# Seven block products in place of eight in part of MLP1's first GEMM

## The chip, the cores and the metric

The kernel runs on one core of one Trainium2 chip. The metric is the device time of one execution in microseconds (us). TensorE (PE) multiplies, VectorE (DVE), ScalarE (ACT) and GpSimd (POOL) work on elements, and SyncE (SP) issues most transfers. SBUF and PSUM are the memories on the core; the eight PSUM banks (512 f32 columns on 128 partitions each) receive the products.

## The reference

Retention over 768 steps in 16 heads (two batches of eight) feeds two MLPs on 1536 tokens of width 512, with a hidden width of 2048:

```
state = gamma * state + k_t v_t^T ;  y_t = scale * q_t @ state          # per head
h = x @ w1_in  ; sp = log1p(exp(min(h, 20))) (h where h > 20)
x2 = (h * tanh(sp)) @ w1_out                                            # MLP1
h = x2 @ w2_in ; out = (h * cos(h)) @ w2_out                            # MLP2
```

All tensors are f32.

## The kernel before

**Retention** runs in six chunks of 128 tokens for each of the two batches: scores (L331), their mask (L337, DVE), the update of the state (L347), the new state `st` (L356, DVE), and the outputs in PSUM (L372, L382). POOL makes the decayed values `vd` (L309) and queries `qd` (L318, L321). ACT writes the high part of the outputs as `x` (L392), DVE the low part (L395).

**The MLPs.** An f32 operand is split into a high and a low part of a type that TensorE multiplies at full rate, and each product is made of three terms (high·high, high·low, low·high). An MLP is worked in four groups of 512 hidden columns and three tiles `j` of 512 tokens. For a group and a tile, `gemm1` (L419) makes h in four column slices of 128 (48 matmuls), two slices together being a *pair* of two banks; Mish (L456, ACT), the high part (L486, ACT) and the low part (L490, DVE) make `g`; `gemm2` (L447) multiplies it by the group's second weight (48 matmuls), and the result is added to `acc` (L506, DVE).

**Weights** come as items: `w(i,G,u)` is half u of group G's part of the first weight, `w(o,G,u)` of the second. An item is loaded into `raw` (L210, SP) and split: absolute value (`mag`; L215 on ACT for the first item, else L222 on DVE), clamp (L228), exponent (L232), rounded high value with its sign (L238), copy of the high part (L250, ACT), the difference (L256, DVE) and the low part (L264, on DVE for the early items, later on POOL). The early items are split in two halves, n0 and n1, of 128x512 each; two `raw` buffers exist, so item k+2 is loaded once item k's low part is done.

**Order.** A class `Plan` list-schedules all operations by costs written beside them and issues each engine's instructions in that order. Engines work in order; on the chip an instruction waits only for semaphores of the data and buffers that it touches. `hold(a, b)` gives the planner a time before which `a` is not placed; it makes no semaphore. Names of buffers in the trace: `bank` is PSUM, `wi` and `wo` weights.

Of the kernel before, what the change touches and what calls it, by code (L numbers as in the profile page):

```python
# [34 lines left out]
    (("x", 2, 0), ("x", 2, 1)), (("wi", 1), ("wi", 2)), (("g", 0), ("g", 1)),  # L35
    (("wo", 0), ("wo", 1)), (("wo", 2), ("g", 2)), (("wi", 2), ("g", 0)),
# [10 lines left out]
TERMS = ((0, 0), (0, 1), (1, 0))  # L47

# [126 lines left out]
def retention_two_mlps(ctx: ExitStack, tc: tile.TileContext, qkv, w1i, w1o, w2i, w2o, consts, out):  # L175
# [9 lines left out]
    t_p = ctx.enter_context(tc.tile_pool(name="t", bufs=3))  # L185
# [207 lines left out]

    def att_x_low(c, b):
        nc.vector.tensor_sub(out=x_chunk(c, b, 1), in0=att_y(c, b), in1=x_chunk(c, b, 0).bitcast(F32))  # L395


# [5 lines left out]
    g_t = {}  # L403

# [48 lines left out]
    def mish(k, fs=slice(0, 2)):  # L453
        if fs.start == 0:
            t_t[k] = t_p.tile([128, 2, BLK], F32, tag="t", name="mish")
        nc.scalar.activation(out=t_t[k][:, fs], in_=h_of(k, fs), func=AF.Mish)  # L456


    def cos_turns(k):
        t_t[k] = t_p.tile([128, 2, BLK], F32, tag="t", name="turns")  # L460
        nc.scalar.activation(out=t_t[k], in_=h_of(k), func=AF.Identity, scale=INV_2PI, bias=quarter)  # L461

    def cos_whole(k):
        n_t[k] = k_p.tile([128, 2, BLK], F32, tag="k", name="whole")
        nc.scalar.activation(out=n_t[k], in_=t_t[k], func=AF.Identity, bias=magic)  # L465

    def cos_angle(k):
        t = t_t[k]
        nc.vector.scalar_tensor_tensor(  # L469
            out=t, in0=n_t[k], scalar=MAGIC, in1=t, op0=ALU.subtract, op1=ALU.subtract  # L470
        )

    def cos_clamp(k):
        t = t_t[k]
        nc.vector.tensor_scalar(out=t, in0=t, scalar1=-0.5, scalar2=0.5, op0=ALU.max, op1=ALU.min)  # L475

    def cos_sin(k):
        nc.scalar.activation(out=t_t[k], in_=t_t[k], func=AF.Sin, scale=-TWO_PI)  # L478

    def g_mul(k):  # L480
        nc.vector.tensor_mul(out=t_t[k], in0=t_t[k], in1=h_of(k))  # L481

    def g_high(k, late):
        n = len(g_t) % 5
        g_t[k] = (late_p if late else g_p).tile([128, 2, 2, BLK], F32R, tag="g%d" % n, name="g")
        nc.scalar.copy(out=g_t[k][:, :, 0, :], in_=t_t[k])  # L486

    def g_low(k):
        g = g_t[k]
        nc.vector.tensor_sub(out=g[:, :, 1, :], in0=t_t[k], in1=g[:, :, 0, :].bitcast(F32))  # L490
# [38 lines left out]
    at = {"gs": []}  # L529

    def weight(it, between=lambda: None):
        raw, mag, w = ("raw", it), ("mag", it), ("w", it)
        first, single = it == ("i", 0, 0), it[:2] in (("i", 0), ("o", 0), ("i", 1))
# [6 lines left out]
        for load, ns in zip(loads, [slice(0, 1), slice(1, 2)] if single else [slice(0, 2)]):  # L540
            c = 0.55 if single else 1.0
            new = None if ns.start else (mag, 2)
            if first:
# [30 lines left out]
            for n in range(ns.start, ns.stop):  # L574
                at["w", it, n] = last

# [26 lines left out]

    def chunk_pre(c):
        for b in range(B):
            if c + 1 < NCH:
                vd = ("vd", c, b)
                op(None, 0.0, att_vd_new, c, b, new=(vd, 2, "vd%d" % b))
# [46 lines left out]
    def chunk_inter(c):  # L655
# [6 lines left out]
        for b in range(B):  # L662
# [6 lines left out]
            at["xl", c, b] = low = op("DVE", 0.69, att_x_low, c, b, needs=[high], uses=[y, x])  # L669
            at.setdefault(x, []).append(low)  # L670
            at.setdefault(("high",) + x, []).append(high)

    def tile_in(m, G, j, f, parts=range(KD), only=None):
# [16 lines left out]
        t, g = ("t", k), ("g", k)  # L690
        if m == 0:
            last = op("ACT", 1.06, mish, k, needs=[last, table], new=(t, 3), uses=hs)
        else:
            kk = ("k", k)
            last = op("ACT", 1.12, cos_turns, k, needs=[last], new=(t, 3), uses=hs)
            last = op("ACT", 1.06, cos_whole, k, needs=[last, at["close"]], new=(kk, 2), uses=[t])
            last = op("DVE", 1.27, cos_angle, k, needs=[last], uses=[t, kk])
            last = op("DVE", 0.72, cos_clamp, k, needs=[last], uses=[t])
            last = op("ACT", 1.08, cos_sin, k, needs=[last], uses=[t])
            last = op("DVE", 1.25, g_mul, k, needs=[last], uses=[t] + hs)  # L700
        n = len(at["gs"]) % 5
        at["gs"].append(k)
        last = op(
            "ACT", 1.06, g_high, k, n > 2, needs=[last] + ([at["close"]] if n > 2 else []),
            new=(g, 1, "g%d" % n), uses=[t],
        )
        at["g", k] = op("DVE", 1.27, g_low, k, needs=[last], uses=[t, g])

    def tile_out(m, G, j, d, u, cols=slice(0, DM)):
# [6 lines left out]
            "PE", 0.72 if half else 1.36, gemm2, m, G, j, d, u, cols, needs=[at[w + (0,)], at[g], at["close"]],  # L716
# [10 lines left out]
        if G == 0:  # L727
            last = op("ACT", 1.05, out_first, m, G, j, p, needs=[last], uses=os + [acc], new=None if p else (acc, NJ))
# [12 lines left out]
    acc_p = k_p = late_p = None  # L741
# [6 lines left out]
    def close():  # L748
        nonlocal acc_p, k_p, late_p
        att_stack.close()  # L750
        acc_p = ctx.enter_context(tc.tile_pool(name="acc", bufs=NJ))
        k_p = ctx.enter_context(tc.tile_pool(name="k", bufs=2))
        late_p = ctx.enter_context(tc.tile_pool(name="late", bufs=1))
# [48 lines left out]
    at["close"] = op(None, 0.0, close)  # L802
    op("PE", 5.5, start_up)
# [21 lines left out]
    later = {1: [("o", 0, 0)], 2: [("o", 0, 1)], 3: [("i", 1, 0)], 4: [("i", 1, 1)]}  # L825
# [22 lines left out]
    for c in range(1, NCH):  # L848
        hold(at["xh", c, 1], at["xh", c, 0])
        if 1 < c < NCH - 1:  # L850
            hold(at["vd", c, 0][1], at["xh", c - 1, 1])
            hold(at["vd", c, 1][1], at["vd", c, 0][1])
    for f in range(2):
        for x in terms:
            tile_in(*steps[0], f, whole, x)
    for i, f in ((1, 0), (1, 1), (0, 2), (0, 3), (1, 2), (1, 3)):
        tile_in(*steps[i], f)
    plan.ops[at["close"]]["before"] |= {n for n, o in enumerate(plan.ops) if o["att"]}
    def weights_of(i):
# [78 lines left out]
```

## Time and profile before

| | us |
|---|---|
| median of 3 runs | 571.11 (570.95 to 571.59) |
| profiled execution | 571.46 |
| its span (first to last instruction) | 569.7 |
| TensorE busy | 564.1 (99% of the span) |
| DVE / ACT / POOL busy | 383.7 / 225.4 / 95.7 |

The profiled execution is 1.76 us longer than its span, and 0.35 us longer than the median. The MLPs begin at 44.01 us of the span.

### The profile page before, as it was taken

How to read it: one execution, taken by the hardware profiler on the slowest of the kernel's cores; microseconds unless marked ns; L12 is line 12 of the kernel's file. 1: busy time of each engine (PE TensorE's matmuls, PEld its weight loads, DVE VectorE, ACT ScalarE, POOL GpSimd, SP SyncE). 2: the span in 40 equal slices, each digit the busy share in tenths (PEclk: the TensorE clock that was granted, in tenths of full speed). 3: DMA queues.
4: the chain of work that ended last, by engine and by line, in shares of the span. 5: the costliest groups of instructions: out<-in, count | busy, mean ns of one | idle time of the engine just before them, and what ended most of it. 6: DMA issues, size and time to landing. Idle time of an engine off the chain costs nothing.

```text
span 569.7 us, 7217 instructions
## 1 busy us (share of the span) xinstructions
PE 564.1 (99%) x3052; PEld 469.1 (82%) x3052; DVE 383.7 (67%) x417; ACT 225.4 (40%) x259; POOL 95.7 (17%) x66
## 2 busy tenths in 40 slices
PE   8999999999999999999999999999999999999997
PEld 7888888888888888888888888888888888888886
DVE  6679899652465527563487976898498894765462
ACT  4264443331312302304326466366246354354240
POOL 6760001111110201111101111122010311010000
PEclk9999999999999999999999999999999999999999
DMA  8983054421042100312021120404003100000203
GB/s 291 396 320 147 3 198 171 148 102 47 1 147 75 74 1 4 144 74 75 0 75 74 49 100 1 147 0 148 0 1 147 41 34 2 0 1 0 75 37 112
DMA packets 16160, 49.32 MB, mean 87 GB/s; under 512 B 1792, under 2 KB 2176, under 8 KB 16128
## 3 DMA queue, kind: packets, MB, share of 16 engines
q1 hardware_dynamic: 16128, 48.86, 23.5%
q8 instruction: 24, 0.39, 0.3%
q14 instruction: 8, 0.07, 0.0%
HBM read 45.71 MB, written 3.15 MB: 86 GB/s over the span
## 4 chain that ended last, share of the span: by engine, by line
PE 96%; DMA 3%; SPq 0%; issue 0%; DVE 0%
PE bank L447 46%; PE bank L419 46%; DMA qkv<-qkv_dram 3%; PE bank L372 1%; PE bank L331 1%; PE bank L382 1%; PE bank L347 1%; SPq L296 0%; SPq L758 0%; DVE acc L513 0%
## 5 line engine op out<-in xcount | busy, mean ns | idle before, releaser
L419 PE MATMUL bank<-x,wi 128*128 128x512 f32 x1152 | 264.8, 389 | 0.0
L419 PEld LDWEIGHTS bank<-x,wi 128*128 128x128 f32 x1152 | 216.1, 188 | 45.0 <-issue 0.2
L447 PE MATMUL bank<-wo,g 128*128 128x512 f32 (+2 forms) x588 | 132.7, 385 | 0.0
L447 PE MATMUL bank<-g,wo 128*128 128x512 f32 x576 | 132.3, 389 | 0.0
L447 PEld LDWEIGHTS bank<-wo,g 128*128 128x128 f32 x588 | 109.1, 188 | 22.1
L447 PEld LDWEIGHTS bank<-g,wo 128*128 128x128 f32 x576 | 108.1, 188 | 22.5
L490 DVE TENSOR_TENSOR g<-mish,g 128x1024 fp32r<-128x1024 f32 x24 | 33.5, 1394 | 58.0 <-ACT g L486 57.9
L264 POOL TENSOR_TENSOR wo<-mag,wo 128x1024 fp32r<-128x1024 f32 x14 | 35.5, 2534 | 214.6 <-ACT wo L250 206.8
L506 DVE TENSOR_TENSOR acc<-bank,acc 128x1024 f32<-128x1024 f32 x35 | 42.8, 1222 | 34.6 <-PE bank L447 34.4
L456 ACT ACTIVATE mish<-bank 128x1024 f32<-128x1024 f32 x24 | 24.7, 1029 | 96.5 <-PE bank L419 96.5
L264 POOL TENSOR_TENSOR wi<-mag,wi 128x1024 fp32r<-128x1024 f32 x12 | 30.3, 2527 | 192.9 <-ACT wi L250 192.9
L469 DVE SCALAR_TENSOR_TENSOR turns<-whole,turns 128x1024 f32<-128x1024 f32 x24 | 29.4, 1223 | 44.7 <-ACT whole L465 44.7
L461 ACT ACTIVATE turns<-bank,quarter 128x1024 f32<-128x1024 f32 x24 | 26.7, 1114 | 65.4 <-PE bank L419 65.1
L238 DVE SCALAR_TENSOR_TENSOR mag<-raw,mag 128x1024 uint32<-128x1024 uint32 (+1 forms) x38 | 40.1, 1056 | 1.1
L478 ACT ACTIVATE turns<-turns 128x1024 f32<-128x1024 f32 x24 | 25.5, 1062 | 34.8 <-DVE turns L475 34.6
L490 DVE TENSOR_TENSOR g<-turns,g 128x1024 fp32r<-128x1024 f32 x24 | 33.2, 1383 | 8.0 <-ACT g L486 8.0
L481 DVE TENSOR_TENSOR turns<-turns,bank 128x1024 f32<-128x1024 f32 x24 | 29.2, 1216 | 10.1 <-ACT turns L478 6.8
L256 DVE SCALAR_TENSOR_TENSOR mag<-raw,mag 128x1024 uint32<-128x1024 uint32 x26 | 33.7, 1301 | 0.4
L486 ACT CAST g<-turns 128x1024 fp32r<-128x1024 f32 x24 | 25.1, 1045 | 17.0 <-DVE turns L481 16.9
L250 ACT CAST wi<-mag 128x1024 fp32r<-128x1024 f32 (+1 forms) x20 | 17.5, 874 | 27.5 <-DVE mag L256 22.4
L465 ACT ACTIVATE whole<-turns,magic 128x1024 f32<-128x1024 f32 x24 | 27.7, 1153 | 0.8
L232 DVE TENSOR_SCALAR mag<-mag 128x1024 uint32<-128x1024 uint32 (+1 forms) x38 | 27.0, 710 | 1.1
(51 smaller groups left out, 320.8 us busy)
## 6 DMA issues: line engine op xcount, KB each, us to landing
raw<-w1i_dram SPq DMA_DIRECT2D x16, 512.0 KB, 4.2
raw<-w1o_dram SPq DMA_DIRECT2D x16, 512.0 KB, 4.1
raw<-w2i_dram SPq DMA_DIRECT2D x16, 512.0 KB, 3.7
raw<-w2o_dram SPq DMA_DIRECT2D x16, 512.0 KB, 3.7
qkv<-qkv_dram SPq DMA_DIRECT2D x12, 512.0 KB, 7.7
qkv<-qkv_dram SPq DMA_DIRECT2D x22, 256.0 KB, 7.2
out_dram<-acc SPq DMA_DIRECT2D x11, 256.0 KB, 2.1
out_dram<-acc SPq DMA_DIRECT2D x1, 160.0 KB, 1.8
```

The source lines that it names most:

```text
L232: nc.vector.tensor_scalar(out=a, in0=a, scalar1=3, scalar2=0x3FFFFFF8, op0=ALU.logical_shift_left, op1=ALU.bitwise_and)
L238: nc.vector.scalar_tensor_tensor(out=a, in0=high, scalar=0xC0000000, in1=a, op0=ALU.bitwise_and, op1=ALU.bitwise_or)
L256: nc.vector.scalar_tensor_tensor(out=w_all_of(it, single)[:, ns], in0=raw_t[it][:, ns, :, 0], scalar=29, in1=mag_t[it][:, ns], op0=ALU.log ...
L264: eng.tensor_sub(out=w[:, :, 1], in0=w_all_of(it, single)[:, ns].bitcast(F32), in1=w[:, :, 0].bitcast(F32))
L419: nc.tensor.matmul(h, w[:, f % 2, a, kk * 128 : (kk + 1) * 128], x[:, b, kk, :], start=(a + b + kk == 0), stop=(a == 1 and kk == KD - 1),)
L447: nc.tensor.matmul(ps, lhs, rhs, start=(n == 0), stop=(n == 3 * GF - 1))
L461: nc.scalar.activation(out=t_t[k], in_=h_of(k), func=AF.Identity, scale=INV_2PI, bias=quarter)
L465: nc.scalar.activation(out=n_t[k], in_=t_t[k], func=AF.Identity, bias=magic)
L469: nc.vector.scalar_tensor_tensor(out=t, in0=n_t[k], scalar=MAGIC, in1=t, op0=ALU.subtract, op1=ALU.subtract)
L481: nc.vector.tensor_mul(out=t_t[k], in0=t_t[k], in1=h_of(k))
L490: nc.vector.tensor_sub(out=g[:, :, 1, :], in0=t_t[k], in1=g[:, :, 0, :].bitcast(F32))
L506: nc.vector.tensor_add(out=acc, in0=o_of((m * NG + G, j, p)), in1=acc)
```

## The change

In groups 1 to 3 of MLP1, token tiles 0 and 1 and one pair of column slices are taken as a 2 by 2 block problem with K halved (Winograd's form of Strassen's scheme): seven products of 6 matmuls (L495) take the place of eight (48 matmuls in all). There are six such blocks; tile 2 of these groups and all of group 0 stay as they were. The scheme needs four sums S1 to S4 of blocks of x and four sums T of blocks of each weight item, split in high and low parts like the operands, and additions of the products in PSUM. The core of the diff:

```diff
+WINOGRAD = (
+    ("c", ("x", 0, 0), ("w", 0, 0), False), ("d", ("S", 2), ("T", 2), False), ("a", ("S", 1), ("T", 0), False),
+    ("b", ("S", 3), ("T", 1), False), ("c", ("x", 0, 2), ("w", 0, 2), True), ("a", ("x", 1, 0), ("w", 1, 2), True),
+    ("b", ("x", 1, 2), ("T", 3), True),
+)
...
+    def w_first_differences(it):
+        w = mag_t[it].bitcast(F32)
+        nc.gpsimd.tensor_sub(
+            out=t_of(it)[:, 0:2], in0=w[:, 1].rearrange("p (k n) -> p k n", k=2), in1=w[:, :, 0 : DM // 2]
+        )
...
+    def att_y_copy(c, b):
+        for k in (0,):
+            y_whole(b, k)
+            nc.scalar.copy(out=att["y"][:, b, :, c * C : c * C + C], in_=att_y(c, b))
...
+    def s_op(to, a, b, plus):
+        to, a, b = (tmp[t] if isinstance(t, int) else y_whole(*t) for t in (to, a, b))
+        (nc.gpsimd.tensor_add if plus else nc.gpsimd.tensor_sub)(out=to, in0=a, in1=b)
...
+    def wino(gi, p, n):
+        to, x, w, more = WINOGRAD[n]
+        ps, last = bank[:, WINO_BANK[to], :], len(TERMS) - 1
+        for kk in range(2):
+            for i, (a, b) in enumerate(TERMS):
...
+                nc.tensor.matmul(
+                    ps, lhs, rhs, start=(not more and kk + i == 0), stop=(kk == 1 and i == last), skip_group_check=True
+                )
...
+    def wino_add(to, n, of):
+        to = tmp[3][:, to] if isinstance(to, int) else bank[:, WINO_BANK[to], :]
+        nc.vector.tensor_add(out=to, in0=bank[:, WINO_BANK[of], :], in1=tmp[3][:, n])
...
-    def mish(k, fs=slice(0, 2)):
-        if fs.start == 0:
-            t_t[k] = t_p.tile([128, 2, BLK], F32, tag="t", name="mish")
-        nc.scalar.activation(out=t_t[k][:, fs], in_=h_of(k, fs), func=AF.Mish)
-
+    def mish(k):
+        nc.scalar.activation(out=h_of(k), in_=h_of(k), func=AF.Mish)
...
-            if first:
+            if it[:2] == ("o", 0) or first:
                 at["act", it, ns.start] = last = op("ACT", 0.62, w_abs_act, it, ns.start, needs=[load], new=new, uses=[raw, mag])
...
-    later = {1: [("o", 0, 0)], 2: [("o", 0, 1)], 3: [("i", 1, 0)], 4: [("i", 1, 1)]}
+    later = {1: [("o", 0, 0)], 2: [("o", 0, 1)]}
...
+    s1 = sum_of(1, (1, 0), (1, 2), True)
+    s2 = sum_of(2, 1, (0, 0), False, s1)
+    s3 = sum_of(3, (0, 0), (1, 0), False)
+    s4 = sum_of((0, 2), (0, 2), 2, False, s2)
+    hold(s1, at["w", ("i", 0, 1), 1])
+    hold(s3, s2)
...
+    for G in range(1, NG):
+        mini(G, 0)
+        g_split()
+        tiles_out(0, G - 1, 2)
...
+        mini(G, 1)
+        g_split()
...
+        tiles_out(0, G, 0)
+        tiles_in(0, G, 2, range(GF))
+        tiles_out(0, G, 1)
```

Around it: ACT copies eight chunks of the retention's output as f32 (`y`, L450 of the changed kernel); Mish works in place in PSUM, so that a pair's banks come free after the low part of g instead of after Mish; the absolute values of `w(o,0,0)` and `w(o,0,1)` move from DVE to ACT; the weights of group 1 are loaded later; some SBUF buffers share slots.

**POOL at the end of the retention.** Before, behind the last `vd` and `qd` (`cst` holds the decays), POOL has nothing to do until the first low part of a weight of group 0's second half:

```order
L309 TENSOR_TENSOR vd<-qkv,cst 128x256 [waits DMAHW6_49,Activation_49]
L309 TENSOR_TENSOR vd<-qkv,cst 128x256 [waits DMAHW7_49,Activation_49]
L321 TENSOR_TENSOR qd<-qkv,cst 64x512 [waits DMAHW5_49,PE_49,Pool_49]
L321 TENSOR_TENSOR qd<-qkv,cst 64x512
L264 TENSOR_TENSOR wo<-mag,wo 128x2x512 [waits PE_49,DMAHW0_49,Activation_49,Pool_49]
```

In the changed kernel the four sums (L471; `tmp`, `y` and `uw` are f32 buffers) stand directly behind them:

```order
L360 TENSOR_TENSOR vd<-qkv,cst 128x256 [waits DMAHW7_49]
L368 TENSOR_TENSOR qd<-qkv,cst 128x512 [waits DMAHW3_49]
L471 TENSOR_TENSOR tmp<-y 128x1024 [waits PE_49,Activation_49,Pool_49]
L471 TENSOR_TENSOR tmp<-tmp,y 128x1024 [waits Pool_49]
L471 TENSOR_TENSOR y<-y,tmp 128x1024 [waits Pool_49]
L471 TENSOR_TENSOR uw<-y 128x1024
L484 TENSOR_TENSOR S<-tmp,S 128x1024 [waits DVE_49,PE_49,Activation_49] x2
```

None of the four waits for DVE: the first waits for PE (the last update of the state, whose `vd` had the slot), for ACT (the last `y` copy) and for POOL itself.

**ACT at the first pairs.** Before, behind the splits of the first item, Mish and the high part of g alternate with copies of weights:

```order
L250 CAST wi<-mag 128x512 x2
L456 ACTIVATE mish<-bank 128x1024
L486 CAST g<-mish 128x2x512
L250 CAST wi<-mag 128x512
L456 ACTIVATE mish<-bank 128x1024
L486 CAST g<-mish 128x2x512
L250 CAST wo<-mag 128x512
```

In the changed kernel an absolute value of `w(o,0,0)` stands ahead of the first Mish (L578) and another ahead of the second, each between two table loads:

```order
L267 CAST wi<-mag 128x512
L228 ACT_TABLE_LOAD
L228 ACTIVATE mag<-raw 128x512
L578 ACT_TABLE_LOAD
L578 ACTIVATE bank<-bank 128x1024
L628 CAST g<-bank 128x2x512
L267 CAST wi<-mag 128x512
L228 ACT_TABLE_LOAD
L228 ACTIVATE mag<-raw 128x512
L578 ACT_TABLE_LOAD
L578 ACTIVATE bank<-bank 128x1024
L628 CAST g<-bank 128x2x512
```

A third such stretch follows (load, absolute value, copy of S, absolute value, load, third Mish). The program has nine table loads; before it had three.

**PE in groups 0 and 1.** Before, 48 matmuls of each GEMM alternate from here on:

```order
L419 MATMUL bank<-x,wi 128x512 x48
L447 MATMUL bank<-g,wo 128x512 x48
L419 MATMUL bank<-x,wi 128x512 x48
L447 MATMUL bank<-g,wo 128x512 x48
L419 MATMUL bank<-x,wi 128x512 x48
```

In the changed kernel the first 144 matmuls of gemm1 (now L543) and 96 of gemm2 (now L571) are as they were, and then come the two blocks of group 1, each of seven products:

```order
L543 MATMUL bank<-x,wi 128x512 x144
L571 MATMUL bank<-g,wo 128x512 x96
L495 MATMUL bank<-x,wi 128x512 x6
L495 MATMUL bank<-S,T 128x512 x18
L495 MATMUL bank<-x,wi 128x512 x12
L495 MATMUL bank<-x,T 128x512 x6
L571 MATMUL bank<-g,wo 128x512 x48
L495 MATMUL bank<-x,wi 128x512 x6
L495 MATMUL bank<-S,T 128x512 x18
L495 MATMUL bank<-x,wi 128x512 x12
L495 MATMUL bank<-x,T 128x512 x6
```

A block of two tiles takes 42 matmuls, where two pairs took 48.

## Rows read from the trace of the kernel before

**Rows 1.** The page: busy time of each engine, share of the span, instructions.

```profile
PE 564.1 (99%) x3052; PEld 469.1 (82%) x3052; DVE 383.7 (67%) x417; ACT 225.4 (40%) x259; POOL 95.7 (17%) x66
```

**Rows 2.** Chain of waits: start us, length us, engine, buffer, line, instructions.

```profile
44.01 32.88 PE bank L419 x144
...
98.65 10.88 PE bank L419 x48
...
544.73 22.13 PE bank L447 x108
566.88 0.36 DVE acc L513
```

**Rows 3.** Timeline, 38 to 55 us: start, length, operation, [idle before, releaser].

```profile
38.94 1.10 PE L347 MATMUL bank<-vd,qkv 128*64 128x64 f32 x32
...
40.70 0.68 DVE L238 SCALAR_TENSOR_TENSOR mag<-raw,mag 128x512 uint32<-128x512 uint32 x1
...
45.67 0.69 DVE L264 TENSOR_TENSOR wi<-raw,wi 128x512 fp32r<-128x512 f32 x1 [0.50 <-ACT wi L250]
...
46.39 7.57 SPq L210 DMA_DIRECT2D raw<-w1o_dram  x4
...
49.73 1.03 ACT L456 ACTIVATE mish<-bank 128x1024 f32<-128x1024 f32 x1 [1.18 <-PE bank L419]
...
54.84 1.22 DVE L490 TENSOR_TENSOR g<-mish,g 128x1024 fp32r<-128x1024 f32 x1
```

**Rows 4.** Timeline where DVE and POOL work together: 380 us, 96 us.

```profile
379.94 1.22 DVE L238 SCALAR_TENSOR_TENSOR mag<-raw,mag 128x1024 uint32<-128x1024 uint32 x1
379.98 3.44 POOL L264 TENSOR_TENSOR wo<-mag,wo 128x1024 fp32r<-128x1024 f32 x1 [8.92 <-ACT wo L250]
...
381.19 3.30 DVE L256 SCALAR_TENSOR_TENSOR mag<-raw,mag 128x1024 uint32<-128x1024 uint32 x1
...
95.86 2.48 POOL L264 TENSOR_TENSOR wo<-mag,wo 128x1024 fp32r<-128x1024 f32 x1 [56.14 <-ACT wo L250]
96.13 2.77 DVE L232 TENSOR_SCALAR mag<-mag 128x1024 uint32<-128x1024 uint32 x1
```

**Rows 5.** Groups by line and shape, DVE: busy us, mean ns of one.

```profile
L256 DVE SCALAR_TENSOR_TENSOR mag<-raw,mag 128x1024 uint32<-128x1024 uint32 x26 | 33.7, 1301 | 0.4
L238 DVE SCALAR_TENSOR_TENSOR mag<-raw,mag 128x1024 uint32<-128x1024 uint32 x26 | 31.8, 1224 | 0.8
L232 DVE TENSOR_SCALAR mag<-mag 128x1024 uint32<-128x1024 uint32 x26 | 21.9, 841 | 0.7
L228 DVE TENSOR_SCALAR mag<-mag 128x1024 f32<-128x1024 f32 x26 | 18.0, 692 | 0.5
L222 DVE TENSOR_SCALAR mag<-raw 128x1024 uint32<-128x1024 uint32 x26 | 17.4, 687 | 3.9 <-POOL wo L264 3.8
L337 DVE TENSOR_TENSOR p<-bank,cst 128x512 f32<-128x512 f32 x24 | 15.0, 682 | 3.1 <-PE bank L331 3.1
```

**Rows 6.** The same view, POOL and ACT.

```profile
L264 POOL TENSOR_TENSOR wo<-mag,wo 128x1024 fp32r<-128x1024 f32 x14 | 35.5, 2534 | 214.6 <-ACT wo L250 206.8 <-DMA raw<-w1o_dram 7.8
L486 ACT CAST g<-mish 128x1024 fp32r<-128x1024 f32 x24 | 25.2, 1050 | 1.3 <-PE bank L447 0.6
L250 ACT CAST wi<-mag 128x512 fp32r<-128x512 f32 x8 | 5.0, 620 | 5.1 <-DVE mag L238 5.1
```

**Rows 7.** Timeline: ACT's first absolute value of n1 and a table load.

```profile
38.05 0.69 ACT L215 ACTIVATE mag<-raw 128x512 f32<-128x512 f32 x1 [0.78 <-DMA raw<-w1i_dram]
38.77 1.28 ACT L451 ACT_TABLE_LOAD   x1
```

**Rows 8.** Loads into `raw` issued from 40 to 62 us: issue to landing.

```profile
DMA to landing us min/median/max: 3.2/3.7/4.1
```

**Rows 9.** Timeline of PE at the program's start (matmuls of zeros).

```profile
1.06 5.30 PE L793 MATMUL bank<-zero 128*128 128x256 bf16 x24 [1.06 <-DVE magic L798]
...
8.52 1.06 PE L793 MATMUL bank<-zero 128*128 128x256 bf16 x8
```

More of the change, by code (lines that the diff above doesn't have):

```diff
@@ L669, in chunk_inter @@
             at["xl", c, b] = low = op("DVE", 0.69, att_x_low, c, b, needs=[high], uses=[y, x])
+            if c < 4:
+                at["yc", c, b] = op("ACT", 0.58, att_y_copy, c, b, needs=[high], uses=[y])
             at.setdefault(x, []).append(low)
@@ L689, in tile_in @@
             return
-        t, g = ("t", k), ("g", k)
+        g = ("g", k)
         if m == 0:
[L692 to L707, printed above, removed]
+            at["g"].append((k, [op("ACT", 1.06, mish, k, needs=[last, table], uses=hs)], hs))
+            return
+        n = len(at["cos"])
+        at["cos"].append(k)
+        t, kk = ("t", k), ("k", k)
@@ L859, in weights_of @@
[L859 to L881 removed]
+            tile_in(0, 0, 0, f, whole, x)
@@ new lines, in retention_two_mlps, with sum_of @@
+    g_split()
+    tiles_in(0, 0, 1, (0, 1))
+    tiles_in(0, 0, 0, (2, 3))
+    last_j1 = len(plan.ops)
+    tiles_in(0, 0, 1, (2, 3))
+    j1_done = [n for n in range(len(plan.ops)) if plan.ops[n]["fn"] is gemm1 and plan.ops[n]["args"][2] == 1]
+    new = op(None, 0.0, s_new, needs=[at["ret"]], new=[("S", 1, "S2"), ("tmp", 1, "T")])
+    plan.lines["UW"], plan.lines["S1"], plan.lines["S3"] = ["S"], ["S"], ["S"]
+    sums = ["S", "tmp"]
+    def sum_of(to, a, b, plus, *after):
+        return op("POOL", 2.0, s_op, to, a, b, plus, needs=[new, *after], uses=sums)
@@ new lines, in split_of @@
+    def split_of(n, last, *after):
+        uses = sums + ([("x", 0, 1)] if n == 4 else [])
+        high = op("ACT", 1.05, s_high, n, needs=[last, *after], uses=uses)
+        at["S", n] = [op("POOL", 2.4, s_low, n, needs=[high], uses=uses)]
+    s1 = sum_of(1, (1, 0), (1, 2), True)
[4 more added lines that the diff above has]
+    hold(s3, s2)
+    for n, last in ((2, s2), (1, s1), (3, s3)):
+        split_of(n, last)
@@ L883, in retention_two_mlps @@
+    at["t"] = op(None, 0.0, t_new, new=[("turns", 1, "S2"), ("turns2", 1, "UW"), ("whole", 1, "S3")])
+    plan.lines["S1"] = ["S"]
+    free_g.append(4)
+    last = (0, NG - 1, 2)
+    for i, step in enumerate(steps[NG * NJ :]):
+        m, G, j = step
+        if j < 2:
+            weights_of(m * NG + G, j)
+        tiles_in(*step, range(GF))
+        tiles_out(*last, by_pairs)
+        last = step
+    tiles_out(*last, in_the_end)
     with tc.manual_schedule():
```

301 lines of the change are left out of this document (229 added, 72 removed).

## The prediction

> **What bounds the kernel now.** I read the page's busy times first: TensorE works 564.1 of 569.7 us [rows 1]. The chain of waits says the same in order of time: from 44.01 us to 566.86 us it is PE alone, one GEMM phase of 48 matmuls after another at 10.88 us, so 226.7 ns per matmul, and 0.36 us of DVE end it [rows 2]. No other engine is near its limit on average. So a matmul less is 226.7 ns less, as long as what PE reads is ready and its banks are free. The place where this is tightest is found in the timeline behind 44 us: PE begins the MLPs while the first weight item is still being split on DVE (n0's and n1's operations run from 40.70 to 46.36 us), and the load of `w(o,0,0)` goes out at 46.39, when the first `raw` is free [rows 3].
>
> **What the change removes.** Six blocks of 48 matmuls become 42: 36 x 226.7 ns = **-8.16 us** on PE [rows 2].
>
> **The sums and DVE.** The four sums (128x1024 on POOL) stand directly behind the retention's last `qd`, and none waits for DVE. The planner's `hold` places them behind the split of `w(i,0,1)` in its plan only. Their last release is the end of PE's last update: 38.94 + 1.10 = 40.04 us [rows 3]. So they run from about 40.1 us, just when DVE has to make n0 and n1 of the first item. I price a sum by POOL's low part of the same size, 2534 ns, less some waiting in that mean: 2.4 to 2.5 us [rows 6].
>
> What does such an operation do to DVE? The rows at 380 us show both engines wanting their SBUF operands at once: L238 runs 1.22 us undisturbed, POOL's L264 is issued at 379.98 and shows 3.44 us, its own 2.4 plus a wait for L238's end; then L256, next on DVE, shows 3.30 us in place of some 1.2. At 96 us L232 shows 2.77 us where its mean is 0.84 [rows 4, 5]. So one operation waits for the whole of the other, and the one that asked first goes next: POOL got in between two neighbours on DVE. With four sums back to back each lets one DVE operation through: first sum 40.1 to 42.5, L256's part of n0 to 43.2; second to 45.6, clamp of n1 to 46.0; third to 48.4, exponent of n1 to 48.9; fourth to 51.3, rounding of n1 to 52.0 (DVE operations at 0.4 to 0.7, as at 128x512 in [rows 3]). Then low n0 ends at 52.7, difference and low n1 at 54.0. Without the sums, in this order, low n1 would end at 45.4: **8.6 us late**. PE's first pair needs low n0 in its third term, after 8 matmuls at 45.8 us, and low n1 two matmuls later; so PE stands still until 54.0 and is 7.7 us late (54.0 + 0.45 of the two matmuls against 46.72).
>
> The Trainium skill, SBUF — State Buffer, section "Who interferes with whom", calls the port pair that DVE and GpSimd share an exclusive lock, taken by DVE operations with two SBUF inputs or in a 2-port mode. The trace agrees in [rows 4]; the page doesn't say who gets it next.
>
> **The table loads on ACT.** The order shows six more ACT_TABLE_LOADs around the absolute values of `w(o,0,0)` and `w(o,0,1)`, now on ACT. One takes 1.28 us and starts at once behind the operation before it [rows 7]. ACT works in order, so the first Mish stands behind a transfer. The first `raw` comes free with low n1 (54.0), the load lands 3.2 us later at best [rows 8]: 57.3. Load of the table 58.6, absolute value (0.69) 59.3, table 60.5, Mish (1.03) 61.6, high part (1.05) 62.6, low part on DVE (1.22) 63.85 [rows 3, 6, 7]. Mish now works in the banks, so only then are the first pair's banks free for the third pair: PE starts it at 64.0, where it was 44.01 + 48 x 0.2267 = 54.9: 9.1 us late, already more than the 7.7 above. The fourth pair waits for copy 0.62, load 1.28, absolute value 0.69, load 1.28, Mish, high, low from 62.6 on: 70.0 (before 60.3). The fifth waits for two copies of S (1.05 each), two absolute values, two loads, Mish, high, low from 68.7 on: 78.2 (before 65.8). From there on ACT has no such stretch, and the pairs follow PE again: group 0's first GEMM ends at 89.3 in place of 76.89. In all PE loses **12.4 us**, some 8.6 by the sums and 3.8 by ACT. Two absolute values on ACT save DVE's L222 there, which is on nobody's path.
>
> The Trainium skill, ScalarE: Activation LUTs, section "Table sets: the hidden batching unit", says that cheap functions such as abs are in every set. By that no load would be needed between Abs and Mish, and the time would be that of the third rival below. The trace shows one behind an absolute value, ahead of Mish's first use [rows 7], and the order has them in the program; that each costs its 1.28 us there, no row shows.
>
> **PE's clock.** At the start 24 small matmuls took 5.30 us (221 ns each), and 8 later ones 1.06 us (133 ns) [rows 9]: the lower level (1.2 GHz) and most of the higher (2.4). A pause of 8 us may bring the lower one back. At worst the first 24 units of work afterwards cost 24 x 88 ns = 2.1 us more; the first two pairs would end at 64.7 in place of 62.6, where the third waits for ACT until 64.0 anyway. I take 0, bound 0.7.
>
> **What lies beside other work.** The eight `y` copies (as the 0.62 us copies, [rows 6]) stand on ACT in the retention, where PE waits for transfers: 0, at most 0.6 if the last of them delays the last chunk. In each block the seven products take 1.36 us each. The first add into a bank that PE returns to must be done in the two products between (2.72 us), and costs 0.68 as L337, which reads PSUM likewise [rows 5]: 2.0 us to spare; the next, 1.8. The T parts of an item (POOL 1.3, 0.6, 0.6, 2.5; ACT 1.05) come out about 3 us before their block in group 1 and 8 in the others. The four copies and low parts of S run until about 85 us, before their first use at about 111. MLP2 and the tail keep their order: 0.
>
> The narrowest place is the second half of `w(o,G,·)`: its `raw` is free only after the low part of T. From there, landing 3.7 (up to 4.1), DVE 0.69 + 0.69 + 0.84 + 1.22 + 1.30, copy 1.05, POOL 2.53 make 12.0 us [rows 5, 6, 8], where I count 14.4 until PE asks for it. I take 0; with two more waits like those of [rows 4] it is 2 to 3 us in each of three groups.
>
> **The sum.** 571.46 - 8.16 + 12.4 = 575.7 for an execution like the profiled one, which is 0.35 over the median of the runs: **575.3 us**. Its own range: the landings 3.2 to 4.1, each sum 2.3 to 2.5, the order in which the two engines get in (one operation of 0.7 more or less in two places) and the clock: 573.5 to 577.5.
>
> **The rivals.**
> - *DVE gets through* (faster, the other side). If DVE, whose operations follow each other within 0.1 us, keeps its operands until low n1 is done, POOL waits instead and nobody needs the sums before 62 us. Only ACT's 3.6 us stay (load out at 45.4, landing 48.6; third pair at 55.3, fifth at 69.4 against 65.8): 571.46 - 8.16 + 3.6 - 0.35 = 566.6. It speaks for it that the sums also wait for each other; against it, that L264 got in between L238 and L256 [rows 4]. It decides below 8.16 - 3.6 = 4.6 us of delay: when at most one sum of four gets in ahead.
> - *Half of it.* Two sums get in ahead: 3.6 + 4.3 = 7.9 us lost, 570.9 and so no change to speak of.
> - *The table loads cost nothing*, because none is needed between an absolute value and Mish, or because it is done during the wait for the transfer. With the sums in the way as above, PE is late by the 7.7 us of low n1: 571.46 - 8.16 + 7.7 - 0.35 = 570.7, the same. (The first of these reasons is the rule of the page ScalarE: Activation LUTs of the Trainium skill, cited above.)
> - *Neither costs:* 571.11 - 8.16 = 563.0.
> - *The second halves of w_out late as well:* 575.3 + 5 = 580, if the 2.4 us to spare go in two groups.
> - That fewer matmuls are not run is excluded by the order: 42 stand where 48 were.
>
> **How the numbers follow.** The forecast has 0.62, for its two prices are in rows and nothing in the program orders the sums behind DVE. DVE through 0.11, half of it 0.10, table loads for nothing 0.07, neither 0.04, the halves late 0.06. Two runs of this kernel differ by up to 0.1%, so 0.2%, 1.1 us, is what a measurement can tell. Faster: 0.11 + 0.04 and 0.03 of the two cases near no change = 0.18; the same: 0.10 of them; slower: 0.62 + 0.06 and the last 0.04 of them = 0.72. For 8 in 10 the range takes the forecast's own (0.62), the two near 571 (0.17), and needs one more: down to 566.4 for DVE getting through; it leaves out 563 and 580. Range 566.4 to 578.0.
>
> **What the profile after would show** (lines of the changed kernel). Right: four L471 on POOL from about 40.1 to 51.3, and single operations of DVE among them at 2.8 to 3.1 us; PE's largest gap, some 8 us, at about 46, its end by DVE's low n1; gaps ahead of the third, fourth and fifth pair that end with L632 at about 64, 70 and 78; six more table loads of 1.28 us; the first gemm2 near 89; from there no gap, and seven products of 1.36 us in each block. Wrong: sums that show 5 us and more while DVE's rows stay at 0.4 to 0.7; PE without a gap near 46; a block that waits for L504 or L308; gaps at gemm2 that end with L281 on POOL.

## The result and the profile after

The changed kernel takes **575.56 us** (median of 20 runs, 574.08 to 576.69), the kernel before, run between them, 571.49 us (20 runs, 570.42 to 574.67). The ratio is 1.0067, 95% interval 1.0055 to 1.0078: 0.67% slower. The forecast was 575.3 us. The profiled execution took 574.17 us, 1.4 below the median, with a span of 572.5 us; what it adds up to is its own time. In the profiles of this study the MLPs begin between 43.34 (e4) and 45.95 us (e1), so the retention alone differs by up to 2.6 us between them. Of the 20 runs, the eight with a mean granted clock of 0.990 or 0.991 have a median of 575.9 us, the other twelve (0.993 to 0.997) one of 574.75; what sets the one or the other isn't shown.

The page of the changed kernel, busy time of each engine, answers to [rows 1]:

```profile
PE 557.9 (97%) x3016; PEld 462.9 (81%) x3016; DVE 416.9 (73%) x441; ACT 252.9 (44%) x315; POOL 155.2 (27%) x100
```

36 matmuls are gone, yet PE's busy time fell by 6.2 us, not by 8.16, and its share of the span fell: it waits now, and part of its work runs slower. The chain of waits of the changed kernel says where not to look (start, length, engine, line, instructions; compare [rows 2]):

```profile
76.60 11.19 PE bank L543 x48
87.79 21.76 PE bank L571 x96
109.55 9.52 PE bank L495 x42
119.07 10.88 PE bank L571 x48
...
547.47 22.13 PE bank L571 x108
```

From 87.79 us on every phase follows the one before it at once, a block at 9.52 us where two pairs had 10.88. From the first gemm2 to the end of PE's work it is 569.60 - 87.79 = 481.81 us; before it was 566.86 - 76.89 = 489.97. The difference is the whole -8.16 us. All that was lost lies ahead: the first gemm2 comes 44.3 us after the MLPs' start (43.46), where it came 32.9 after.

The timeline of the changed kernel from 39.5 to 52.8 us, the place of [rows 3] (start, length, operation, [idle before, releaser]; L471 are the sums):

```profile
39.75 2.74 POOL L471 TENSOR_TENSOR tmp<-y 128x1024 f32<-128x1024 f32 x1
40.17 0.68 DVE L404 TENSOR_TENSOR st<-bank,cst 128x512 f32<-128x512 f32 x1
...
40.77 2.26 DVE L273 SCALAR_TENSOR_TENSOR raw<-raw,mag 128x512 uint32<-128x512 uint32 x1
...
42.57 2.72 POOL L471 TENSOR_TENSOR tmp<-tmp,y 128x1024 f32<-128x1024 f32 x1
42.96 2.61 DVE L241 TENSOR_SCALAR mag<-mag 128x512 f32<-128x512 f32 x1
...
45.36 2.40 POOL L471 TENSOR_TENSOR y<-y,tmp 128x1024 f32<-128x1024 f32 x1
45.60 2.44 DVE L245 TENSOR_SCALAR mag<-mag 128x512 uint32<-128x512 uint32 x1
47.73 2.52 POOL L471 TENSOR_TENSOR uw<-y 128x1024 f32<-128x1024 f32 x1
48.08 2.71 DVE L251 SCALAR_TENSOR_TENSOR mag<-raw,mag 128x512 uint32<-128x512 uint32 x1
50.71 0.68 DVE L281 TENSOR_TENSOR wi<-raw,wi 128x512 fp32r<-128x512 f32 x1
...
51.45 23.01 PE L543 MATMUL bank<-x,wi 128*128 128x512 f32 x88 [5.87 <-DVE wi L281]
```

Four operations of DVE that took 0.4 to 0.7 us take 2.3 to 2.7, one for each sum, and PE waits 5.87 us for the low part that comes behind them. L404, which has one operand in PSUM, runs its usual 0.68 us beside the first sum. Then ACT, from 56 to 63 us of the same timeline:

```profile
56.12 1.28 ACT L228 ACT_TABLE_LOAD   x1 [0.64 <-DMA raw<-w1o_dram]
57.42 0.71 ACT L228 ACTIVATE mag<-raw 128x512 f32<-128x512 f32 x1
58.15 1.28 ACT L578 ACT_TABLE_LOAD   x1
59.44 1.01 ACT L578 ACTIVATE bank<-bank 128x1024 f32<-128x1024 f32 x1
60.52 1.01 ACT L628 CAST g<-bank 128x1024 fp32r<-128x1024 f32 x1
...
61.57 1.22 DVE L632 TENSOR_TENSOR g<-bank,g 128x1024 fp32r<-128x1024 f32 x1 [2.27 <-ACT g L628]
...
62.85 5.31 PEld L543 LDWEIGHTS bank<-x,wi 128*128 128x128 f32 x24 [0.40 <-DVE g L632]
...
68.72 5.31 PEld L543 LDWEIGHTS bank<-x,wi 128*128 128x128 f32 x24 [0.56 <-DVE g L632]
```

The first Mish stands behind the two loads, and the third pair behind the low part of the first g (L632). The same view has the fifth pair at 76.60 with 2.14 us of waiting in front. Last, TensorE's granted clock by stretch (length, busy us and instructions of PE, PEld, DVE, ACT, POOL, then the clock, the DMA share and GB/s):

```profile
44.00:51.40 7.40, 1.58 (x7) 0.94 (x5) 7.33 (x5) 0.52 (x1) 6.17 (x3) 0.84 0.00 0
51.40:62.50 11.10, 11.05 (x40) 8.96 (x40) 8.48 (x15) 7.93 (x11) 0.00 (x0) 0.80 0.26 94
62.50:76.60 14.10, 11.82 (x51) 8.86 (x49) 9.25 (x13) 13.94 (x16) 5.34 (x2) 1.00 0.20 75
```

Behind its wait PE worked the first two pairs at a mean granted clock of 0.80, so for part of the stretch at the lower level (1.2 of 2.4 GHz): from 51.45 until about 62.45 us for the 40 matmuls that were left of them, which take 9.1 us at 226.7 ns.

### The profile page after: what moved, and what is told of

Read it like the earlier page. It is cut to its first block, busy times and chain, and to the rows that moved or that the text cites. A ratio compares the mean times of both kernels' runs of the same rounds, so it can differ in the third digit from the quotient of the medians.

```text
span 572.5 us, 7317 instructions
## 1 busy us (share of the span) xinstructions
PE 557.9 (97%) x3016; PEld 462.9 (81%) x3016; DVE 416.9 (73%) x441; ACT 252.9 (44%) x315; POOL 155.2 (27%) x100
## 4 chain that ended last, share of the span: by engine, by line
PE 89%; issue 4%; POOL 4%; DMA 2%; DVE 0%; SPq 0%; POOLq 0%
PE bank L571 46%; PE bank L543 30%; PE bank L495 10%; DMA qkv<-qkv_dram 2%; PE bank L381 1%; PE bank L420 1%; POOL tmp L471 1%; POOL S L484 1%; PE bank L395 1%; PE bank L430 1%; POOL uw L471 0%; POOL y L471 0%; POOL qd L371 0%; POOL qd L368 0%; DVE g L632 0%
## 5 line engine op out<-in xcount | busy, mean ns | idle before, releaser
L543 PE MATMUL bank<-x,wi 128*128 128x512 f32 x864 | 201.8, 393 | 8.2 <-DVE wi L281 5.9
L543 PEld LDWEIGHTS bank<-x,wi 128*128 128x128 f32 x864 | 163.3, 190 | 44.0 <-DVE wi L281 6.3
L571 PE MATMUL bank<-wo,g 128*128 128x512 f32 (+2 forms) x588 | 132.7, 385 | 0.0
L571 PE MATMUL bank<-g,wo 128*128 128x512 f32 x576 | 132.3, 389 | 0.0
L571 PEld LDWEIGHTS bank<-wo,g 128*128 128x128 f32 x588 | 109.1, 188 | 22.1
L571 PEld LDWEIGHTS bank<-g,wo 128*128 128x128 f32 x576 | 108.1, 188 | 22.5
L281 POOL TENSOR_TENSOR wi<-mag,wi 128x1024 fp32r<-128x1024 f32 x14 | 37.0, 2643 | 111.3 <-ACT wi L267 111.3
L251 DVE SCALAR_TENSOR_TENSOR mag<-raw,mag 128x1024 uint32<-128x1024 uint32 (+1 forms) x36 | 44.0, 1224 | 0.7
L632 DVE TENSOR_TENSOR g<-turns,g 128x1024 fp32r<-128x1024 f32 x24 | 36.8, 1532 | 8.3 <-ACT g L628 8.3
L632 DVE TENSOR_TENSOR g<-bank,g 128x1024 fp32r<-128x1024 f32 x12 | 14.7, 1222 | 29.4 <-ACT g L628 26.1
L241 DVE TENSOR_SCALAR mag<-mag 128x1024 f32<-128x1024 f32 (+1 forms) x36 | 31.3, 874 | 1.3 <-ACT mag L228 0.4
L245 DVE TENSOR_SCALAR mag<-mag 128x1024 uint32<-128x1024 uint32 (+1 forms) x36 | 31.3, 874 | 0.5
```

The source lines that it names most:

```text
L241: nc.vector.tensor_scalar(out=a, in0=a, scalar1=F64_HIGH, scalar2=F64_LOW, op0=ALU.min, op1=ALU.max)
L245: nc.vector.tensor_scalar(out=a, in0=a, scalar1=3, scalar2=0x3FFFFFF8, op0=ALU.logical_shift_left, op1=ALU.bitwise_and)
L251: nc.vector.scalar_tensor_tensor(out=a, in0=high, scalar=0xC0000000, in1=a, op0=ALU.bitwise_and, op1=ALU.bitwise_or)
L281: eng.tensor_sub(out=w[:, :, 1], in0=w_all_of(it, single)[:, ns].bitcast(F32), in1=w[:, :, 0].bitcast(F32))
L543: nc.tensor.matmul(h, w[:, f % 2, a, kk * 128 : (kk + 1) * 128], x[:, b, kk, :], start=(a + b + kk == 0), stop=(a == 1 and kk == KD - 1),)
L571: nc.tensor.matmul(ps, lhs, rhs, start=(n == 0), stop=(n == 3 * GF - 1))
```

## The experiments

The theory: the sums take from DVE the access to SBUF that both engines need, one DVE operation per sum, and the six table loads come on top on ACT. The ratios are to runs of the kernel before from the same rounds.

**e1_fence: the sums wait for DVE.** POOL first copies one column of the last low part of `w(i,0,1)`, so that the hold of the plan is one on the chip too.

```diff
+    def s_wait(n, it, h):
+        nc.gpsimd.tensor_copy(out=tmp[n][:, 0, 0:1], in_=w_t[it][:, h, 1, 0:1].bitcast(F32))
...
-    s1 = sum_of(1, (1, 0), (1, 2), True)
+    wait = op("POOL", 0.1, s_wait, 1, ("i", 0, 1), 1, needs=[new, at["w", ("i", 0, 1), 1]], uses=sums + [("w", ("i", 0, 1))])
+    s1 = sum_of(1, (1, 0), (1, 2), True, wait)
```

> The four sums made to wait for DVE's last low part of w(i,0,1) (a copy of one column from it ahead of the first sum on POOL); the order on all engines else is that of the changed kernel. Theory (the sums take DVE's SBUF port and so delay the first low parts; ACT's table loads come on top): low n1 of the first item back at about 45.4, no gap of PE near 46, third pair at about 55.5 and fifth at about 69.5; total 566 to 568 us. Rival 1 (ACT's stretch with the absolute values sets the end whatever DVE does): third pair stays near 62.8, total about 575.5. Rival 2 (the sums cost as much wherever they stand): a gap of PE of 5 us or more between 56 and 75, total 572 or more.

Measured: 572.39 us (12 runs, 570.96 to 574.02), ratio 1.0008 (0.9996 to 1.0020). The gap near 46 is gone, as the theory had it, but its 566 to 568 us were missed. The total is the second rival's (572 or more), though not with its one gap of 5 us or more: four shorter ones add up to 5.7 us. The timeline from 64 to 74 us shows what the four sums and the low parts of S (L487 here) do in their new place; L635 is the low part of g:

```profile
69.00 5.35 POOL L487 TENSOR_TENSOR S<-tmp,S 128x1024 fp32r<-128x1024 f32 x2
69.25 2.88 DVE L251 SCALAR_TENSOR_TENSOR mag<-raw,mag 128x512 uint32<-128x512 uint32 x1
...
72.05 1.21 DVE L635 TENSOR_TENSOR g<-bank,g 128x1024 fp32r<-128x1024 f32 x1
...
73.31 7.37 PE L546 MATMUL bank<-x,wi 128*128 128x512 f32 x24 [2.12 <-DVE g L635]
```

L251 waits for POOL, g's low part (ready since ACT's high part at 70.4) waits behind L251 in DVE's order, and the fifth pair waits for it, since with Mish in place the banks are free only then. PE's four gaps (0.93, 1.66, 2.12 and 1.00 us) and a fifth pair that took 7.37 us where the others took 5.74 make the first gemm2 come 41.5 us after the MLPs' start: 8.6 us lost, where I had expected 3.6. L635 itself takes its usual 1.21 us with POOL at work beside it: one of its operands is in PSUM, and it is late only by its place in the order.

**e2_dve_abs: the absolute values back on DVE**, the sums where they were.

```diff
-            if it[:2] == ("o", 0) or first:
+            if first:
```

> The absolute values of w(o,0,0) and w(o,0,1) back on DVE, so three table loads in the program; the sums stay where they were. Theory: PE's gap near 46 stays (low n1 at about 52.8), the third pair follows the second without a wait, and only this gap of 6.5 to 7.7 us is lost: 569.8 to 571.0 us if PE's clock costs nothing; with the 24 and more matmuls at the lower clock behind the gap, which ACT no longer hides, 2.4 us more, 572.2 to 573.4. Rival (the table loads cost nothing): 575.5 as before the edit. Rival (ACT is the whole loss): 563.

Measured: 571.48 us (12 runs, 570.01 to 572.55), ratio 0.9998 (0.9987 to 1.0009), so 4.1 us less than the changed kernel. Its PE timeline:

```profile
51.86 33.21 PE L543 MATMUL bank<-x,wi 128*128 128x512 f32 x136 [5.52 <-DVE wi L281]
```

The gap near 46 stays (5.52 us), none follows, and the 136 matmuls behind it take 33.21 us where 30.8 are usual (granted clock 0.80 over the first 11 us): the loss is the gap and the clock, 40.8 us to the first gemm2 in place of 32.9. The time lies between the two ranges that the theory gave, without and with the clock, and so in neither.

**e3_both: both edits.**

> Both edits: the sums wait for w(i,0,1) and the absolute values are on DVE. Theory: the two causes are all that was lost; PE without a gap behind the retention, 571.5 - 8.2 = 563.3 us, and up to 564.5 if the sums, now beside the split of w(o,0,0), delay something there. Rival (the block itself, its adds or the second halves of w_out cost something too): 565.5 or more, with gaps of PE behind 100 us.

Measured: 566.58 us (5 runs, 565.97 to 566.68), ratio 0.9910 (0.9894 to 0.9926). Faster than both kernels, but 2 us above the theory's bound, with the rival's size and not its place: no gap lies behind 100 us. Two gaps (1.89 and 0.15 us) stand at the fifth and sixth pair, again behind a low part of g that waits in DVE's order behind an operation held up by POOL. The windows from 44 to 77 us (columns as above) say why no place there is free; the kernel before:

```profile
44.00:77.00 33.00, 33.00 (x147) 27.30 (x147) 30.22 (x52) 15.39 (x20) 0.00 (x0) 1.00 0.26 96
```

and e3:

```profile
44.00:77.00 33.00, 30.96 (x134) 24.63 (x133) 32.59 (x32) 16.15 (x19) 20.57 (x9) 1.00 0.18 64
```

DVE was busy for 30.2 of 33 us there before, with POOL idle. With POOL busy for 20.6 us, DVE shows 32.6 us, waits within its operations included, and has done 32 operations of much the same list where it had done 52.

**e4_before_four and e5_before_two: the sums alone**, as additions that nothing uses, in the kernel before.

```diff
+    def att_fill():
+        scratch = att_p.tile([128, 2 * BLK], F32, tag="fill", name="fill", bufs=1)
+        for _ in range(4):
+            nc.gpsimd.tensor_add(out=scratch, in0=att[3, 0][:, 0:1024], in1=att[3, 1][:, 0:1024])
...
+    pool_last = [at["qd", NCH - 1, b] for b in range(B)] + [at["vd", NCH - 2, b][0] for b in range(B)]
+    op("POOL", 0.1, att_fill, needs=pool_last, uses=[chunk(3, 0), chunk(3, 1)])
```

> The kernel before with four additions of 128x1024 on POOL behind the last qd; their result is used by nothing, and nothing else is changed. Theory (the port alone delays DVE): each lets one operation of DVE through, low n1 at about 53 to 54.7, PE's gap 7 to 8.4 us: 578.5 to 580 us, and 2.4 more if PE's clock falls behind the gap, to 582.5. Rival (DVE goes on between them, or POOL waits): 571.5 to 573.

> As e4_before_four (the kernel before with additions on POOL behind the last qd), with two additions in place of four. Theory (each lets one DVE operation through, and only the operations up to low n0 count): the two hold up the rounding and the difference of n0, low n0 at about 46.5, PE's gap 1 to 1.5 us and too short for its clock to fall: 572.3 to 573 us. Rival (the loss goes with the number of additions, half of e4's 7.5): 575 us.

Measured: 578.94 us with four (4 runs, 578.43 to 579.93; ratio 1.0132, 1.0113 to 1.0151) and 573.37 with two (7 runs, 572.37 to 575.36; ratio 1.0040, 1.0023 to 1.0056). Timeline of e4, where L329 are the additions:

```profile
39.29 10.39 POOL L329 TENSOR_TENSOR fill<-qkv 128x1024 f32<-128x1024 f32 x4
...
40.10 2.10 DVE L238 SCALAR_TENSOR_TENSOR mag<-raw,mag 128x512 uint32<-128x512 uint32 x1
...
42.23 2.76 DVE L256 SCALAR_TENSOR_TENSOR raw<-raw,mag 128x512 uint32<-128x512 uint32 x1
...
44.91 2.57 DVE L228 TENSOR_SCALAR mag<-mag 128x512 f32<-128x512 f32 x1
47.51 2.45 DVE L232 TENSOR_SCALAR mag<-mag 128x512 uint32<-128x512 uint32 x1
49.88 0.68 DVE L264 TENSOR_TENSOR wi<-raw,wi 128x512 fp32r<-128x512 f32 x1
...
50.62 2.93 PE L424 MATMUL bank<-x,wi 128*128 128x512 f32 x6 [5.14 <-DVE wi L264]
```

Nothing but these four operations was added, no buffer of theirs is one that DVE reads there, and the four DVE operations beside them wait as they did in the changed kernel. That is the mechanism by itself. The PE timelines of e4 and e5, over the rest of group 0's first GEMM:

```profile
50.62 33.80 PE L424 MATMUL bank<-x,wi 128*128 128x512 f32 x136 [5.14 <-DVE wi L264]
...
47.14 31.53 PE L424 MATMUL bank<-x,wi 128*128 128x512 f32 x136 [1.19 <-DVE wi L264]
```

In e4 the gap is 5.14 us where the theory had 7 to 8.4, and the lower clock behind it costs 3.0 us more (33.80 in place of 30.8): the time lies in the range of 578.5 to 580 us, which was given without the clock, because these two misses about cancel. With two, PE's gap is 1.19 us and the granted clock behind it 1.00, and the loss is not half of four's: 2.1 of 7.5 us. 573.37 us is 0.4 above the theory's range and far from the rival's 575.

**e6_cut and e7_fence_cut: the same work in pieces.** Sums and low parts of S in four pieces each, on e2 and on e3.

```diff
-        (nc.gpsimd.tensor_add if plus else nc.gpsimd.tensor_sub)(out=to, in0=a, in1=b)
+        for k in range(2):
+            for q in (slice(0, 256), slice(256, BLK)):
+                (nc.gpsimd.tensor_add if plus else nc.gpsimd.tensor_sub)(out=to[:, k, q], in0=a[:, k, q], in1=b[:, k, q])
```

> As e2_dve_abs (absolute values on DVE, sums where the change put them), but each of the four sums and of their low parts on POOL is issued in four pieces of 128x256; the work is the same. Theory (one operation on POOL lets one of DVE through, so what a DVE operation waits is the length of one POOL operation): DVE operations wait 0.6 us each in place of 2.4, low n0 at about 47.5 in place of 51.4, PE's gap near 46 at 1 to 2 us in place of 5.5: 567.5 us, or 565 if PE's clock then stays up, and up to 568.5 if the second item's low parts come late instead. Rival (the port is lost for the sums' whole time, however they are cut): 571.5 as e2_dve_abs.

> As e3_both (the sums wait for w(i,0,1), the absolute values on DVE), with sums and their low parts cut in four pieces as in e6_cut. Theory: the waits for banks before the fourth and fifth pair, which come from a low part of g behind a DVE operation that waits for a whole sum, shrink from 2 us to 0.6: 564 to 565.5 us, the fastest of all. Rival (cutting changes nothing, since DVE and POOL are full together between 44 and 77 us): 566.6.

Measured: e6 570.79 us (11 runs, 569.57 to 571.61; ratio 0.9982, 0.9968 to 0.9995), outside what the theory gave; e7 565.15 us (4 runs, 564.90 to 565.80; ratio 0.9892, 0.9876 to 0.9907), within it. Timeline of e6:

```profile
43.90 1.10 DVE L251 SCALAR_TENSOR_TENSOR mag<-raw,mag 128x512 uint32<-128x512 uint32 x1
44.41 4.63 POOL L473 TENSOR_TENSOR tmp<-tmp,y 128x256 f32<-128x256 f32 x4
44.92 1.22 DVE L281 TENSOR_TENSOR wi<-raw,wi 128x512 fp32r<-128x512 f32 x1
...
60.37 23.98 PE L547 MATMUL bank<-x,wi 128*128 128x512 f32 x96 [4.80 <-DVE g L636]
```

DVE's operations now wait 0.4 to 0.5 us, low n0 ends at 46.1 us, and PE has no gap there: what a DVE operation waits goes with the length of one POOL operation. But the sums last until 57 us and meet nearly all of the second item's split, so that the first pair's g is late: 4.80 us ahead of the third pair, behind which 96 matmuls take 23.98 us where 21.8 are usual. The loss moved by one item; cutting alone returned 0.7 us. In e7, where the sums stand behind both items, it returned 1.4. What e7 still loses stands in its PE timeline, at the second halves of gemm2:

```profile
82.52 0.73 PE L578 MATMUL bank<-g,wo 128*128 128x512 f32 x2 [0.18 <-ACT wo L267]
84.28 16.16 PE L578 MATMUL bank<-g,wo 128*128 128x512 f32 x70 [1.02 <-DVE wo L281]
```

**e8_copy: ACT's order without the loads.** A copy in place of the absolute value of `w(o,0,0)` and `w(o,0,1)`.

```diff
+        if it[0] == "o":
+            nc.scalar.copy(out=to, in_=of)
+        else:
+            nc.scalar.activation(out=to, in_=of, func=AF.Abs)
```

> The changed kernel with a plain copy on ACT in place of the absolute value of w(o,0,0) and w(o,0,1), which leaves the absolute value out; ACT's order is the same and it waits for the same transfers, but the program has three table loads in place of nine. Theory (the six loads are the 4 us between this kernel and e2_dve_abs): third pair at PE's own pace, 570.5 to 572.5 us. Rival (Mish waits because it stands behind a transfer in ACT's queue, with or without loads): 574 to 575.5.

Measured: 570.95 us (12 runs, 570.33 to 572.62), ratio 0.9995 (0.9985 to 1.0006). 4.6 us less than the changed kernel with the transfer still in ACT's order. ACT and PE of e8 (L230 the copy, L580 Mish):

```profile
56.08 0.69 ACT L230 COPY mag<-raw 128x512 f32<-128x512 f32 x1 [0.69 <-DMA raw<-w1o_dram]
58.12 1.01 ACT L580 ACTIVATE bank<-bank 128x1024 f32<-128x1024 f32 x1 [1.36 <-PE bank L545]
...
51.35 33.93 PE L545 MATMUL bank<-x,wi 128*128 128x512 f32 x136 [5.71 <-DVE wi L283]
```

The first Mish now waits for PE and not for the copy, and the third pair follows at once: the table loads are the price, not the place in the queue.

**e9_warm, e11_after_warm, e13_after_warm: PE kept at work in its gap** with matmuls of zeros, in e2 (e9) and in the changed kernel (e11, e13). In e9 and e11 the zeros overwrite a part of the last chunks' outputs in PSUM before their low parts are taken.

```diff
+    def warm():
+        for _ in range(40):
+            nc.tensor.matmul(bank[:, 6, 0:256], zero, zero[:, 0:1].to_broadcast([128, 256]), start=True, stop=True)
...
+            if f == 0 and x is terms[1]:
+                op("PE", 0.01, warm)
```

> As e2_dve_abs, with 40 matmuls of zeros (256 columns, into a bank that is free) on PE behind the first 8 matmuls, so that PE works through most of its wait for low n0. If the 136 matmuls behind the gap take 33.2 us in place of 30.8 because PE's clock fell in it: the granted clock stays at 1.00, 30.8 us, and 569.1 us in all. If the clock costs nothing at the end: 571.5.

> The changed kernel with 40 matmuls of zeros (256 columns, into bank 7, which is free by then) on PE behind the first 8, so that its clock doesn't fall. If the fall costs nothing in the changed kernel, as the prediction took it, because ACT holds the third pair until about 62.8 anyway: 575.5 us, with the clock at 1.00 from 44 to 60 us. If it costs there what it costs in e2_dve_abs: 573.

> As e11_after_warm, whose zeros came too late since ACT still read bank 7; here they go into bank 3, which nothing uses between the masks and the second pair. If the clock's fall costs nothing in the changed kernel because ACT holds the third pair until about 62.8: 575.5 us, clock 1.00 from 44 to 60. If it costs what it costs in e2_dve_abs: 573.

Measured: e9 571.37 us (12 runs, 569.05 to 572.93; ratio 0.9992, 0.9978 to 1.0006); e11 578.12 (4 runs; ratio 1.0117, 1.0100 to 1.0134); e13 575.78 (6 runs, 573.41 to 578.67; ratio 1.0073, 1.0048 to 1.0099). e11 says nothing of the clock: the zeros waited for ACT's last copy of x and came at 52.72 us, behind the gap, where they only delayed PE. In e9 and e13 they stand in the gap. Windows of e13, as above:

```profile
44.00:60.00 16.00, 14.73 (x86) 11.97 (x85) 14.87 (x18) 6.11 (x8) 6.16 (x3) 1.00 0.17 66
60.00:90.00 30.00, 27.09 (x111) 21.62 (x110) 21.98 (x28) 22.82 (x26) 10.62 (x4) 0.94 0.19 71
```

The clock stayed up from 44 to 60 us. PE then waits 1.95 us ahead of the third pair, which starts at 62.77 us where it started at 62.85, and the time and the first gemm2 (87.72 us) are those of the changed kernel: there the fall costs nothing. In e9's profile the 136 matmuls take 31.19 us in place of 33.21, so the fall was worth 2.0 us in that place, but that execution is the fastest of its 12. The mean granted clock was 0.997 to 1.000 in all runs of e9 and 0.993 or 0.994 in all of e2, and yet e9's median is only 0.1 below e2's, within the spread of both: that the end gains the 2.0 us is not shown.

**e12_fence_twice: the best version.** As e7, and the low parts of S3 and S4 wait until DVE is done with `w(o,0,1)`.

```diff
+    def s_low_wait(n, it, h):
+        nc.gpsimd.tensor_copy(out=s_parts(n)[1][:, 0, 0:1], in_=w_t[it][:, h, 1, 0:1])
...
+        if n == 3:
+            at["S wait"] = op(
+                "POOL", 0.1, s_low_wait, n, ("o", 0, 1), 1, needs=[high, at["w", ("o", 0, 1), 1]], uses=uses + [("w", ("o", 0, 1))]
+            )
```

> As e7_fence_cut, with the low parts of S3 and S4 made to wait in the same way until DVE has made the last low part of w(o,0,1). Theory (what e7 still loses, 1.2 us ahead of gemm2's second halves and what follows, is DVE held up by these pieces): PE without a gap up to group 1's first block, 563.3 to 564.3 us. Rival (w(o,0,1) is late by DVE's own work, or the low parts of S3 and S4 come too late for the block): 565 or more.

Measured: **563.34 us** (4 runs, 562.74 to 563.73), ratio 0.9858 (0.9843 to 0.9874): 1.4% faster than before, 2.1% below the changed kernel's median. Its PE timeline:

```profile
44.10 32.98 PE L553 MATMUL bank<-x,wi 128*128 128x512 f32 x144
76.91 21.92 PE L581 MATMUL bank<-g,wo 128*128 128x512 f32 x96
98.67 1.52 PE L505 MATMUL bank<-x,wi 128*128 128x512 f32 x6
```

PE has no gap from the MLPs' start to the first block. What the blocks save is then the whole change: 571.25 - 8.16 = 563.1.

## Why the prediction was right

**What PE saves: right to the last digit.** -8.16 us between the first gemm2 and the end, and six blocks of 9.52 us without a wait inside. The adds, the T parts and the second halves of w_out are hidden as I had them; the rival of late halves is out.

**The sums and DVE: the mechanism right, the gap mis-sized.** The four sums ran from 39.75 to 50.24 us (40.1 to 51.3 expected), one DVE operation waited for each (2.3 to 2.7 us, where I had 2.8 to 3.1), and low n1 ended at 52.79 (54.0). e4 shows the mechanism by itself, e6 that it goes by the length of one operation. The step that failed in size: "low n1 two matmuls later; so PE stands still until 54.0". PE resumes with low n0 (51.4); n1 holds the second column slice, whose third term is 12 matmuls behind. So the gap is 5.87 us and ends with low n0, where I had PE 7.7 us late by low n1. It made no difference to the end, since ACT held the third pair. The Trainium skill, SBUF — State Buffer, section "Who interferes with whom", has the exclusive lock that these rows show.

**ACT: right.** Pairs three, four and five were expected 9.1, 9.7 and 12.4 us late; they began at 62.85, 68.72 and 76.60, and the first gemm2 11.4 us late by the MLPs' start. That is 1.0 below the sum's 12.4, as low n1 came 1.2 us earlier. ACT's part, 3.8 expected, measures 4.1 (e2) and 4.6 (e8), with what the clock costs there in both, and e8 puts it on the loads. By the rule of the page ScalarE: Activation LUTs (Trainium skill, "Table sets: the hidden batching unit") no load would be needed between an absolute value and Mish; this program had them, at 1.28 us each, and the rival built on it gave 570.7, where e8 without the loads takes 570.95. That agreement is luck in part: the rival had PE 7.7 us late and the clock at nothing, and e8 has a gap of 5.71 us and 3.1 us by the clock.

**The clock: nothing at the end, for the reason given, but too small a worst case.** It fell, the 40 matmuls left of the first two pairs took 11.0 us in place of 9.1, and e13 shows that the end doesn't move by it, since ACT is later still. The margin was thin: PE was through at 62.45 us and the third pair's banks came free at 62.85. The 2.1 us "at worst", from 24 small matmuls at the start, doesn't hold behind such gaps: the 136 matmuls took 2.4 (e2), 3.0 (e4) and 3.1 us (e8) more than 30.8.

**The other side, "DVE gets through", is out:** the sums went ahead each time. But its price, 566.6 us for ACT's stretch alone, was too low as well. e1 has no gap at 46 and still takes 572.4. I had looked at where the sums stand, not at how much room there is: the windows of e3 show the 44 to 77 us in which some 10 us of sums and as much of low parts meet a DVE that had 2.8 us to spare before. That had no part in the forecast, since the sums were where they hurt at once, but it is why e1 and e3 missed.

**The sum** was 575.7 for an execution like the profiled one before, and the profiled one after took 574.17: 0.5 less by an earlier start of the MLPs, 1.0 by the smaller loss. The median of 20 runs lies 1.4 above this profile. So a part of the agreement with 575.3 is chance, about 1 us; what makes the other executions longer is not in a profile here (their granted clocks are given above).

## What to carry to other kernels

A planner's hold that no semaphore enforces is a wish: read from the built order what an instruction waits for before trusting where it stands. Work on GpSimd is not free merely because GpSimd is idle: where DVE has all its operands in SBUF, each of its operations may wait for a whole one of GpSimd's, so add both engines' times in the stretch, keep the pieces short, and make them wait until the operations on PE's path are through. And when a buffer is released later than before (here PSUM behind g's low part), everything ahead of the releasing instruction in its engine's order has become PE's business.

## What was not expected of the hardware

Behind waits of 5.1 to 5.9 us the granted clock was 0.74 (e4) and 0.80 (changed kernel) over the next 11 us. Shorter waits did not do the same each time: behind 2.12 us in e1 it was 0.80 from 73.3 to 81.7 us, behind 2.14 us in the changed kernel 1.00 from 76.6 to 87.8. And GpSimd and DVE took turns strictly in the changed kernel and in e4: between two of the four additions exactly one operation of DVE got through. Those of its operations that have an operand in PSUM didn't wait (L404 0.68 us in the changed kernel, L635 1.21 us in e1).
